# Dense layer pair with Silu: x transposes alone on SyncE's queue, w1 loads on ScalarE's

## The chip, the cores and the metric

The kernel runs on one core of a Trainium2 chip. The metric is the device time of one execution in microseconds. The median of three runs before the change is 126.39 us (125.19 to 127.03).

The engines: TensorE multiplies (in the profile PE, its weight loads PEld), ScalarE (ACT) does Silu and half of the copies out of PSUM, VectorE (DVE) the other copies, SyncE (SP) issues DMAs. ScalarE can issue DMAs too. SP's DMAs and ScalarE's go through two queues to the same 16 DMA engines. GpSimd (POOL) only sets four constants.

## The reference

```python
B, S, D, F = 1, 2048, 640, 1728     # bf16
h = einsum("bsd,df->bsf", x, w1)
h = silu(h)
out = einsum("bsf,fd->bsd", h, w2)
```

## The kernel before

x has 2048 rows of 640 values. The kernel cuts the rows into four chunks of 512, the 640 contraction columns into five tiles of 128 (index k), and the 1728 features into 13 tiles of 128 (index ft) and a rest of 64. The first product needs x with its contraction on the partitions, so x is loaded from memory by DMA transposes (`turn_x`, L107) into `xT`. w1 is loaded into `w1s` by plain copies (`load_w1`, L104), w2 into `w2s` and `w2t`.

The first stage has this order on TensorE:

- 13 dummy matmuls on a zeroed tile `z` (L134 to L137), 256 columns each, with no data from memory.
- The opening, chunk 0 with feature tiles 0 to 7 (L182 to L189): for each k, eight matmuls of 512 columns, one into each of the eight PSUM banks. So each k needs one tile of x (`ld_x[k]`, L184) and 1024 columns of w1 (`ld_w[k, 0]` and `ld_w[k, 1]`, L186). After the last k each bank goes through Silu on ScalarE (L169).
- The rest of chunk 0, feature tiles 8 to 12, with the five k of one bank in a row (L190 to L196). It waits for `ld_wr` (L146), the load of the w1 columns from 1024 on, 880 KB: the w1 remainder.
- Chunks 1 to 3, 13 feature tiles each, each behind its transpose `ld_xc[c]` (L147, L191), then the feature rest (L198 to L204).

All matmuls of both products are recorded on line L165. The second product follows from 64 us on, with transposes and stores issued by SP (L249 to L317); the change doesn't touch it.

What orders the start is a start barrier: each engine reports to it with a Drain and waits for its release at an EventSemaphore. `early` (L89) moves instructions ahead of one of the two: with `arrived` False ahead of the engine's Drain, so that they delay its report, with True between Drain and EventSemaphore, where they go on while others have not reported. Before the change these are moved so:

- SP: `x0(0, 2)`, the transpose of x tiles 0 and 1 of chunk 0, ahead of the Drain (L118); behind the Drain `sp_front` (L122 to L129), in this order: w1 tile k=0 second half, w1 k=1, x tiles 2 and 3, w1 k=2, w1 k=3, x tile 4, w1 k=4. After the barrier follow the w1 remainder, the transposes of chunks 1 to 3 and four w2 loads (L146 to L153).
- ScalarE: the first half of w1 tile k=0 (L132), behind its Drain; after the barrier a small Silu on a zeroed tile (L143, L144), which brings the load of the activation table with it.
- VectorE: the two memsets (L119, L120), ahead of its Drain.
- TensorE: the dummies, behind its Drain (L141). The opening comes after the barrier.

Each DMA has a semaphore of its own (`dma_sem`), and all matmuls that report share `s_pe`.

Of the kernel before, what the change touches and what calls it, by code (L numbers as in the profile page):

```python
# [5 lines left out]
ACT = mybir.ActivationFunctionType  # L6
ET = mybir.EngineType


def bass_standalone__dense_activation_silu__prompt_kernel(  # L10
# [12 lines left out]
    F = w1.shape[1]  # L23
    P = 128
    NB = 8
    BANK = 512
    DT = D // P
# [7 lines left out]
    FO = 8  # L35
    assert (S, D, F) == (2048, 640, 1728) and FL == 64

    pe, act, dve, sp = nc.tensor, nc.scalar, nc.vector, nc.sync

    with ExitStack() as es:  # L40
        def sb(name, shape, dtype):
            return es.enter_context(nc.sbuf_tensor(name, shape, dtype))

        xT = sb("xT", [P, DT, S], bf16)
        w1s = sb("w1s", [P, DT, F], bf16)
# [6 lines left out]
        z = sb("z", [P, 256], bf16)  # L52
        zw = sb("zw", [P, 8], fp32)
        ps = es.enter_context(nc.psum_tensor("ps", [P, NB, BANK], fp32))
# [3 lines left out]
        def sem(name):  # L58
            return [es.enter_context(nc.semaphore(name)), 0]

        def tick(ins, s, n=1):
            ins.then_inc(s[0], n)
            s[1] += n
            return (s, s[1])

        def wait(eng, *points):
            for pt in points:
                if pt is None:
                    continue
                s, v = pt  # L70
                key = (id(eng), id(s))
                if seen.get(key, 0) < v:
                    eng.wait_ge(s[0], v)
                    seen[key] = v

        s_pe, s_act, s_dve = sem("s_pe"), sem("s_act"), sem("s_dve")
        n_dma = [0]

        def dma_sem():
            n_dma[0] += 1  # L80
            return sem(f"s_dma{n_dma[0]}")

        def load(eng, out_ap, in_ap):
            return tick(eng.dma_start(out=out_ap, in_=in_ap), dma_sem(), 16)
# [4 lines left out]
        def early(emit, engine, arrived):  # L89
            lst = nc.main_func.blocks[0].instructions  # L90
            n = len(lst)
            r = emit()
            lst = nc.main_func.blocks[0].instructions
            new = lst[n:]
            del lst[n:]
            op = "EventSemaphore" if arrived else "Drain"
            at = next(i for i, ins in enumerate(lst) if ins.opcode == op and ins.engine == engine)
            lst[at:at] = new
            return r

        w1_v = w1.rearrange("(dt p) f -> p dt f", p=P)
        w2_v = w2[0:F0, :].rearrange("(ft p) d -> p ft d", p=P)

        def load_w1(eng, k, a, b):  # L104
            return load(eng, w1s[:, k, a * P:b * P], w1_v[:, k, a * P:b * P])

        def turn_x(c, k0, k1):  # L107
            return turn(sp, xT[:, k0:k1, c * SCH:(c + 1) * SCH],
                        xf[c * SCH:(c + 1) * SCH, k0 * P:k1 * P])

        ld_x, ld_w = {}, {}

        def x0(k0, k1):
            r = turn_x(0, k0, k1)
            for k in range(k0, k1):
                ld_x[k] = r

        early(lambda: x0(0, 2), ET.SP, False)  # L118
        p_z = early(lambda: tick(dve.memset(z[:, :], 0.0), s_dve), ET.DVE, False)  # L119
        p_zw = early(lambda: tick(dve.memset(zw[:, :], 0.0), s_dve), ET.DVE, False)  # L120

        def sp_front():  # L122
            ld_w[0, 1] = load_w1(sp, 0, 4, 8)
            ld_w[1, 0] = ld_w[1, 1] = load_w1(sp, 1, 0, 8)
            x0(2, 4)
            ld_w[2, 0] = ld_w[2, 1] = load_w1(sp, 2, 0, 8)
            ld_w[3, 0] = ld_w[3, 1] = load_w1(sp, 3, 0, 8)
            x0(4, 5)
            ld_w[4, 0] = ld_w[4, 1] = load_w1(sp, 4, 0, 8)  # L129

        def act_front():
            ld_w[0, 0] = load_w1(act, 0, 0, 4)  # L132

        def dummies(n):  # L134
            wait(pe, p_z)
            for _ in range(n):
                pe.matmul(ps[:, NB - 1, 0:256], lhsT=z[:, 0:P], rhs=z[:, :], start=True, stop=True)  # L137

        early(act_front, ET.Activation, True)
        early(sp_front, ET.SP, True)  # L140
        early(lambda: dummies(13), ET.PE, True)  # L141

        wait(act, p_zw)  # L143
        act.activation(out=zw[:, :], in_=zw[:, :], func=ACT.Silu)  # L144

        ld_wr = load(sp, w1s[:, :, FO * P:F], w1_v[:, :, FO * P:F])  # L146
        ld_xc = {c: turn_x(c, 0, DT) for c in range(1, NSC)}  # L147
        ld_w2 = [
            load(sp, w2s[:, 0:7, :], w2_v[:, 0:7, :]),
# [8 lines left out]
        def bank():  # L158
            b = nxt[0] % NB
            nxt[0] += 1  # L160
            wait(pe, bank_free[b])
            return b

        def mm(o, l, r, start, stop, shared=False):
            return pe.matmul(o, lhsT=l, rhs=r, start=start, stop=stop, skip_group_check=shared)  # L165

        def silu(out_ap, b, after):
            wait(act, after)
            r = tick(act.activation(out=out_ap, in_=ps[:, b, :], func=ACT.Silu), s_act)  # L169
            bank_free[b] = r  # L170
            return r

        def hcol(ft, c):
            return hT[:, ft, c * SCH:(c + 1) * SCH]

        def xcol(k, c):
            return xT[:, k, c * SCH:(c + 1) * SCH]

        def w1t(k, ft):
            return w1s[:, k, ft * P:(ft + 1) * P]  # L180

        obank = [bank() for _ in range(FO)]  # L182
        for k in range(DT):
            wait(pe, ld_x[k])  # L184
            for ft in range(FO):
                wait(pe, ld_w[k, ft // 4])  # L186
                ins = mm(ps[:, obank[ft], :], w1t(k, ft), xcol(k, 0), start=(k == 0), stop=(k == DT - 1))
                if k == DT - 1:
                    silu(hcol(ft, 0), obank[ft], tick(ins, s_pe))  # L189
        for c in range(NSC):  # L190
            wait(pe, ld_wr if c == 0 else ld_xc[c])  # L191
            for ft in range(FO if c == 0 else 0, FT):
                b = bank()
                for k in range(DT):
                    ins = mm(ps[:, b, :], w1t(k, ft), xcol(k, c), start=(k == 0), stop=(k == DT - 1))
                h_last = silu(hcol(ft, c), b, tick(ins, s_pe))  # L196
        h_tail = []
        for q in range(NSC // 2):  # L198
            b = bank()
            for k in range(DT):  # L200
                for hh in range(2):
                    ins = mm(ps[hh * FL:(hh + 1) * FL, b, :], w1s[:, k, F0:F], xcol(k, 2 * q + hh),
                             start=(k == 0), stop=(k == DT - 1), shared=True)
# [142 lines left out]
```

## Time and profile before

| what | us |
|---|---|
| median of three runs (lowest, highest) | 126.39 (125.19, 127.03) |
| profiled execution, its own time | 126.76 |
| its span, first to last instruction | 125.3 |
| TensorE matmuls busy | 121.6 (97%) |
| weight loads busy | 55.1 |
| ScalarE busy | 38.3 |
| VectorE busy | 7.6 |
| opening's first matmul starts | 3.70 |
| rest of chunk 0 starts | 14.47 |
| first product's last chunk ends, second product starts | about 64.3 |
| last matmul ends | 123.4 |

The issues on SP's queue in the first microseconds, from its timeline, and the landings from the DMA issues of narrow windows:

| issued at | what | KB | issue took | lands after |
|---|---|---|---|---|
| 0.00 | transpose x tiles 0, 1 | 256 | 1.34 | 3.7 |
| 1.83 | w1 k=0 second half, w1 k=1 | 128, 256 | 0.84 both | 2.9, 3.2 |
| 2.72 | transpose x tiles 2, 3 | 256 | 1.23 | 3.7 |
| 3.99 | w1 k=2, k=3 | 256 each | 1.05 both | 4.3, 4.4 |
| 5.09 | transpose x tile 4 | 128 | 1.15 | 4.5 |
| 6.29 | w1 k=4, w1 remainder | 256, 880 | 1.10 both | 3.9, 7.4 |
| 7.43 | transposes of chunks 1, 2, 3 | 640 each | 14.00 all | 9.9 the first, 5.8 the last |

ScalarE's one load was issued at 0.20 and landed 2.4 us later. Its table load starts at 1.98 and takes 1.28, the small Silu 0.21.

A matmul's busy time contains its drain, which the next one overlaps: the distance from start to start is less than the mean duration. An idle time in brackets behind a group names what ended it. A profile's group can merge instructions of several shapes ("+1 forms").

### The profile page before, as it was taken

The numbers are of one execution on the slowest core, as the hardware profiler recorded it, in microseconds if no ns is written. First come the engines' busy times: TensorE is split into PE (matmuls) and PEld (weight loads), VectorE is DVE, ScalarE is ACT, GpSimd is POOL, SyncE is SP. The second block draws the span as 40 slices with busy tenths as digits, with TensorE's granted clock in tenths as the row PEclk, the third lists the DMA queues.
The fourth block names the chain that finished last, engine by engine and source line by source line (L and its number), as shares of the span: only waits on it lengthen the run. The fifth ranks groups of instructions, "written<-read, shape, count | busy, mean of one in ns | idle before, by whom it ended". The sixth has DMA issues, their size and how long they took to land.

```text
span 125.3 us, 1333 instructions
## 1 busy us (share of the span) xinstructions
PE 121.6 (97%) x587; PEld 55.1 (44%) x587; DVE 7.6 (6%) x13; ACT 38.3 (31%) x66; POOL 0.2 (0%) x4
## 2 busy tenths in 40 slices
PE   8899799999999999999999999999999999999993
PEld 5334344444444444444434444444444444444452
DVE  0000000000000000000002020200004210012021
ACT  3100975555555555555540101010003011010100
POOL 0000000000000000000000000000000000000000
DMA  6999699995000000000000000000001468111113
GB/s 130 230 236 344 146 213 154 274 373 182 0 0 0 0 5 0 3 0 0 0 0 0 5 0 0 0 0 0 0 0 42 89 218 295 52 52 52 52 55 102
DMA packets 18437, 10.35 MB, mean 83 GB/s; under 512 B 13056, under 2 KB 17920, under 8 KB 18432
## 3 DMA queue, kind: packets, MB, share of 16 engines
q1 hardware_dynamic: 18144, 10.08, 31.5%
q10 hardware_dynamic: 288, 0.20, 0.7%
q8 instruction: 4, 0.07, 0.2%
q14 instruction: 1, 0.01, 0.0%
HBM read 4.51 MB, written 2.62 MB: 57 GB/s over the span
## 4 chain that ended last, share of the span: by engine, by line
PE 87%; DMA 6%; ACT 0%; issue 0%
PE ps L165 87%; DMA w1s<-in_w_dram 6%; ACT o_sb L215 0%
## 5 line engine op out<-in xcount | busy, mean ns | idle before, releaser
L165 PE MATMUL ps<-xT,w1s 128*128 128x512 bf16 (+1 forms) x280 | 59.7, 383 | 1.3 <-DMA w1s<-in_w_dram 1.0
L165 PE MATMUL ps<-w2s,hT 128*128 128x512 bf16 (+2 forms) x221 | 45.4, 367 | 0.0
L165 PEld LDWEIGHTS ps<-xT,w1s 128*128 128x128 bf16 (+1 forms) x280 | 26.5, 99 | 34.6 <-issue 1.5
L169 ACT ACTIVATE hT<-ps 128x512 bf16<-128x512 f32 x52 | 30.2, 603 | 29.1 <-PE ps L165 29.0
L165 PEld LDWEIGHTS ps<-w2s,hT 128*128 128x128 bf16 x221 | 20.9, 98 | 24.4 <-issue 1.1
L215 ACT CAST o_sb<-ps 128x512 bf16<-128x512 f32 (+1 forms) x8 | 4.4, 545 | 41.8 <-PE ps L165 41.8
L213 DVE CAST o_sb<-ps 128x512 bf16<-128x512 f32 (+1 forms) x9 | 6.1, 677 | 101.4 <-PE ps L165 101.4
L165 PE MATMUL ps<-hT,w2s 128*128 128x512 bf16 x52 | 11.4, 379 | 0.0
L165 PEld LDWEIGHTS ps<-hT,w2s 128*128 128x128 bf16 x52 | 5.1, 98 | 6.1
L215 ACT CAST oT<-ps 128x512 bf16<-128x512 f32 x2 | 1.1, 589 | 11.4 <-PE ps L165 11.4
L137 PE MATMUL ps<-z 128*128 128x256 bf16 x13 | 3.0, 416 | 0.4 <-DVE zw L120 0.4
L165 PE MATMUL ps<-w2t,hTt 64*128 64x512 bf16 (+2 forms) x17 | 2.3, 367 | 0.0
L137 PEld LDWEIGHTS ps<-z 128*128 128x128 bf16 x13 | 1.8, 142 | 1.1 <-DVE zw L120 0.4
L213 DVE CAST oT<-ps 128x512 bf16<-128x512 f32 x2 | 1.3, 686 | 14.1 <-PE ps L165 14.1
L144 ACT ACT_TABLE_LOAD x1 | 1.3, 1283 | 2.0 <-PEq L331 2.0
L169 ACT ACTIVATE hTt<-ps 128x512 bf16<-128x512 f32 x2 | 1.2, 597 | 1.1 <-PE ps L165 1.1
L165 PEld LDWEIGHTS ps<-w2t,hTt 64*128 64x128 bf16 x17 | 0.6, 94 | 1.6 <-issue 1.3
L165 PE MATMUL ps<-hTt,w2t 64*128 64x512 bf16 x4 | 0.6, 376 | 0.0
L165 PEld LDWEIGHTS ps<-hTt,w2t 64*128 64x128 bf16 x4 | 0.2, 94 | 0.2
L144 ACT ACTIVATE zw<-zw 128x8 f32<-128x8 f32 x1 | 0.2, 208 | 0.0
L119 DVE MEMSET z<- 128x128 uint32 x1 | 0.2, 165 | 0.2 <-issue 0.2
L331 POOL MEMSET const-bfloat16-1.0<- 128x1 bf16 x1 | 0.1, 101 | 0.0
(4 smaller groups left out, 0.4 us busy)
## 6 DMA issues: line engine op xcount, KB each, us to landing
out_dram<-o_sb SPq DMA_DIRECT2D x15, 160.0 KB, 1.9
w2s<-in_w_dram SPq DMA_DIRECT2D x1, 1120.0 KB, 6.7
w1s<-in_w_dram SPq DMA_DIRECT2D x4, 256.0 KB, 4.1
w2s<-in_w_dram SPq DMA_DIRECT2D x1, 960.0 KB, 8.8
w1s<-in_w_dram SPq DMA_DIRECT2D x1, 880.0 KB, 7.4
w2t<-in_w_dram SPq DMA_DIRECT2D x2, 80.0 KB, 8.1
w1s<-in_w_dram ACTq DMA_DIRECT2D x1, 128.0 KB, 2.4
w1s<-in_w_dram SPq DMA_DIRECT2D x1, 128.0 KB, 2.9
```

What stands on the lines that cost most here:

```text
L119: p_z = early(lambda: tick(dve.memset(z[:, :], 0.0), s_dve), ET.DVE, False)
L137: pe.matmul(ps[:, NB - 1, 0:256], lhsT=z[:, 0:P], rhs=z[:, :], start=True, stop=True)
L144: act.activation(out=zw[:, :], in_=zw[:, :], func=ACT.Silu)
L165: return pe.matmul(o, lhsT=l, rhs=r, start=start, stop=stop, skip_group_check=shared)
L169: r = tick(act.activation(out=out_ap, in_=ps[:, b, :], func=ACT.Silu), s_act)
L213: r = tick(dve.tensor_copy(out=out_ap, in_=in_ap), s_dve)
L215: r = tick(act.copy(out=out_ap, in_=in_ap), s_act)
L331: nc = _bacc.Bacc("TRN2", target_bir_lowering=False, num_devices=1)
```

## The change

- SP issues `x0(0, 1)`, `x0(1, 3)` and `x0(3, 5)` one after another, all ahead of its Drain, and no w1 load. After the barrier it waits for the w1 remainder before it issues the transposes of chunks 1 to 3 and the w2 loads.
- ScalarE issues all w1 loads behind its Drain. The first half of k=0 goes at once, all others behind `s_pe` 1, which the fourth dummy now raises. Then, still ahead of the barrier's EventSemaphore, the small Silu with its table load. After the barrier it issues the w1 remainder.
- TensorE runs 12 dummies in place of 13, and the opening's first four k stand ahead of the barrier's EventSemaphore too; the last k comes after it.

```diff
-        early(lambda: x0(0, 2), ET.SP, False)
+        def sp_front():
+            x0(0, 1)
+            x0(1, 3)
+            x0(3, 5)
+
+        def act_front():
+            ld_w[0, 0] = load_w1(act, 0, 0, 4)
+            wait(act, (s_pe, 1))
+            ld_w[0, 1] = load_w1(act, 0, 4, 8)
+            for k in range(1, DT):
+                ld_w[k, 0] = ld_w[k, 1] = load_w1(act, k, 0, 8)
+            act_table()
+
+        def act_table():
+            wait(act, p_zw)
+            act.activation(out=zw[:, :], in_=zw[:, :], func=ACT.Silu)
+
+        def dummies(n):
+            wait(pe, p_z)
+            for i in range(n):
+                ins = pe.matmul(ps[:, NB - 1, 0:256], lhsT=z[:, 0:P], rhs=z[:, :], start=True, stop=True)
+                if i == 3:
+                    tick(ins, s_pe)
+
+        early(sp_front, ET.SP, False)
         p_z = early(lambda: tick(dve.memset(z[:, :], 0.0), s_dve), ET.DVE, False)
         p_zw = early(lambda: tick(dve.memset(zw[:, :], 0.0), s_dve), ET.DVE, False)
-
-        def sp_front():
-            ld_w[0, 1] = load_w1(sp, 0, 4, 8)
-            ld_w[1, 0] = ld_w[1, 1] = load_w1(sp, 1, 0, 8)
-            x0(2, 4)
-            ld_w[2, 0] = ld_w[2, 1] = load_w1(sp, 2, 0, 8)
-            ld_w[3, 0] = ld_w[3, 1] = load_w1(sp, 3, 0, 8)
-            x0(4, 5)
-            ld_w[4, 0] = ld_w[4, 1] = load_w1(sp, 4, 0, 8)
...
         early(act_front, ET.Activation, True)
-        early(sp_front, ET.SP, True)
-        early(lambda: dummies(13), ET.PE, True)
-
-        wait(act, p_zw)
-        act.activation(out=zw[:, :], in_=zw[:, :], func=ACT.Silu)
-
-        ld_wr = load(sp, w1s[:, :, FO * P:F], w1_v[:, :, FO * P:F])
+
+        ld_wr = load(act, w1s[:, :, FO * P:F], w1_v[:, :, FO * P:F])
+        wait(sp, ld_wr)
         ld_xc = {c: turn_x(c, 0, DT) for c in range(1, NSC)}
...
+        def opening(k0, k1):
+            for k in range(k0, k1):
+                wait(pe, ld_x[k])
+                for ft in range(FO):
+                    wait(pe, ld_w[k, ft // 4])
+                    ins = mm(ps[:, obank[ft], :], w1t(k, ft), xcol(k, 0), start=(k == 0), stop=(k == DT - 1))
+                    if k == DT - 1:
+                        silu(hcol(ft, 0), obank[ft], tick(ins, s_pe))
+
+        def pe_front():
+            dummies(12)
+            opening(0, DT - 1)
+
+        early(pe_front, ET.PE, True)
+        opening(DT - 1, DT)
```

More of the change, by code (lines that the diff above doesn't have):

```diff
@@ L116, in x0 @@
                 ld_x[k] = r
-        early(lambda: x0(0, 2), ET.SP, False)
+        def sp_front():
[19 more added lines that the diff above has]
+        early(sp_front, ET.SP, False)
         p_z = early(lambda: tick(dve.memset(z[:, :], 0.0), s_dve), ET.DVE, False)
         p_zw = early(lambda: tick(dve.memset(zw[:, :], 0.0), s_dve), ET.DVE, False)
-        def sp_front():
-            ld_w[0, 1] = load_w1(sp, 0, 4, 8)
-            ld_w[1, 0] = ld_w[1, 1] = load_w1(sp, 1, 0, 8)
-            x0(2, 4)
-            ld_w[2, 0] = ld_w[2, 1] = load_w1(sp, 2, 0, 8)
-            ld_w[3, 0] = ld_w[3, 1] = load_w1(sp, 3, 0, 8)
-            x0(4, 5)
-            ld_w[4, 0] = ld_w[4, 1] = load_w1(sp, 4, 0, 8)
[L131 to L137, printed above, removed]
-        early(act_front, ET.Activation, True)
-        early(sp_front, ET.SP, True)
-        early(lambda: dummies(13), ET.PE, True)
-        wait(act, p_zw)
-        act.activation(out=zw[:, :], in_=zw[:, :], func=ACT.Silu)
-        ld_wr = load(sp, w1s[:, :, FO * P:F], w1_v[:, :, FO * P:F])
+        early(act_front, ET.Activation, True)
+        ld_wr = load(act, w1s[:, :, FO * P:F], w1_v[:, :, FO * P:F])
+        wait(sp, ld_wr)
         ld_xc = {c: turn_x(c, 0, DT) for c in range(1, NSC)}
@@ L182, in bass_standalone__dense_activation_silu__prompt_kernel @@
         obank = [bank() for _ in range(FO)]
[L183 to L189, printed above, removed]
+        def opening(k0, k1):
[11 more added lines that the diff above has]
+        opening(DT - 1, DT)
         for c in range(NSC):
```

## The prediction

> **What bounds the kernel now.** I read the chain of work that ended last first, then the groups of instructions, then TensorE's timeline, then the table of stages, then the DMA issues. The chain is short:
>
> ```profile
> by line: PE ps L165 86.9%; DMA w1s<-in_w_dram 5.9%; ACT o_sb L215 0.2%; issue 0.1%
> 6.94 0.06 issue
> 7.00 7.43 DMA w1s<-in_w_dram
> 14.43 0.05 issue
> 14.47 108.90 PE ps L165 x533
> 123.37 0.02 issue
> 123.40 0.27 ACT o_sb L215
> ```
>
> Columns: start, length, what. From 14.47 us to 123.37 us TensorE works without a break. What comes before 14.47 is the only part in which time can be won: the end moves by as much as that instant moves. It is the landing of one load, the w1 remainder (feature tiles 8 to 13), issued at 7.00.
>
> ```profile
> L165 PE MATMUL ps<-xT,w1s 128*128 128x512 bf16 (+1 forms) x280 | 59.7, 383 | 1.3 <-DMA w1s<-in_w_dram 1.0
> L144 ACT ACT_TABLE_LOAD x1 | 1.3, 1283 | 2.0 <-PEq L331 2.0
> ```
>
> Of all idle time ahead of first-stage matmuls, 1.3 us in total, most ends with a w1 load. TensorE's timeline (start, length, what, idle time before) shows where:
>
> ```profile
> 0.39 2.95 PE L137 MATMUL ps<-z 128*128 128x256 bf16 x13 [0.39 <-DVE zw L120]
> 3.70 4.46 PE L165 MATMUL ps<-xT,w1s 128*128 128x512 bf16 x16 [0.35 <-DMA xT<-in_x_dram]
> 8.39 5.34 PE L165 MATMUL ps<-xT,w1s 128*128 128x512 bf16 x24 [0.23 <-DMA w1s<-in_w_dram]
> 14.47 11.83 PE L165 MATMUL ps<-xT,w1s 128*128 128x512 bf16 x54 [0.74 <-DMA w1s<-in_w_dram]
> ```
>
> 24 matmuls take 5.34 us with a drain of about 0.16 after the last, so one goes every 0.2155 us. The 16 before take 4.46. The weight loads say why: they start at 4.10, 4.53, 4.95 and 5.38, 0.425 apart, and the next 11 take 2.28 us. So the array is slow until about 5.4 us, although the granted clock is recorded as 1.00 throughout: four matmuls at 0.425, twelve at 0.2155. The opening of 40 matmuls at full pace is 8.6 us; it starts at 3.70 and the next stage starts at 14.47, so 2.1 us of that stretch go to the slow start (4 x 0.21 = 0.84), 0.23 and 0.74 of waits, and drains.
>
> The table of stages (columns: window, its length, busy us of PE, PEld, DVE, ACT and POOL, clock, DMA share, GB/s) gives transfer rates:
>
> ```profile
> 9.00:10.00 1.00, 1.00 (x6) 0.49 (x5) 0.00 (x0) 0.00 (x0) 0.00 (x0) 1.00 1.01 306
> 10.00:11.00 1.00, 1.00 (x7) 0.41 (x5) 0.00 (x0) 0.00 (x0) 0.00 (x0) 1.00 1.04 366
> 12.00:13.00 1.00, 1.00 (x7) 0.47 (x5) 0.00 (x0) 0.74 (x2) 0.00 (x0) 1.00 2.77 155
> 13.00:14.00 1.00, 0.73 (x4) 0.12 (x2) 0.00 (x0) 1.00 (x3) 0.00 (x0) 1.00 0.15 31
> 15.00:16.00 1.00, 1.00 (x7) 0.41 (x6) 0.00 (x0) 1.00 (x3) 0.00 (x0) 1.00 1.28 290
> ```
>
> Copies alone (the w1 remainder, 10 to 11) run at 366 GB/s, transposes alone (15 to 16) at 290. Between 13 and 14 only 31 GB/s move: the last packets of the w1 remainder trickle, and the chunk-1 transposes queued behind it hardly advance. That is how a transpose can stand still beside an unfinished copy.
>
> **The change, part by part.** The sum is against the profiled execution: span 125.3, time 126.76, 0.37 above the median of the runs, 126.39. I subtract gains from the median too.
>
> *First transpose of one tile instead of two.* Issues on SP cost 1.34 and 1.23 for two tiles and 1.15 for one (timeline of SP). The two-tile transpose landed 3.7 after its issue at 0. One tile saves about 0.2 of issue and 128 KB, 0.45 us at 290 GB/s: it lands at about 3.0. The floor is TensorE itself: one dummy fewer (2.95 becomes about 2.74 busy, the next instruction can start at 2.95). I take 3.0 instead of 3.70; bounds 2.95 and 3.7. If the clock still steps up at 5.4, contraction tile 0 has 5.6 slow matmuls and 2.4 fast ones: it ends at 5.9 (before: 8 matmuls from 3.70 end at 6.3). Most of the 0.7 us is spent on slow matmuls.
>
> *w1 loads on ScalarE's queue behind dummy 4.* That dummy ends near 0.39 + 4 x 0.213 + drain = 1.4 to 1.5. Then five issues at the 0.42 of the L84 row: 1.5 to 3.6. The first ACT load was issued at 0.20 and landed 2.4 later. So tile 0's second half, issued at 1.5, lands about 3.9, wanted at 3.0 + 4 x 0.425 = 4.7: hidden, and if it took the 4.4 of the slowest small w1 load, 5.9, it would cost 1.2. Tile 1, issued at 1.9, lands between 4.3 and 6.3 (2.4 to 4.4); wanted at 5.9. Tiles 2 to 4 are issued 0.42 apart and wanted 1.72 apart, so they are hidden behind matmuls. All five cost nothing under that cover.
>
> *Transposes alone on SP's queue.* x tiles 1 and 2 are issued at 1.15, tiles 3 and 4 at about 2.4. This is the disputed price, since before has no stretch where long copies and transposes run from two queues. Lower bound: 3.7 from issue as for tiles 0 and 1, so 4.85, hidden behind tile 0. The nearest row is the second transpose of before, landing 3.7 after issue with 384 KB of copies ahead of it in its own queue; beside this one run 640 KB (half of tile 0, tiles 1 and 2), 256 KB or 0.7 us more: 5.6. Upper bound, if the engines give each queue one packet in turn: copies of 1152 KB from 2.5 on are 640 packets and take 3.2 us, 640 of the transpose's 1024 packets go between them (0.57 us), the other 384 after (0.34), plus 0.45 from the last packet to the landing (as for the first transpose: 3.2 and 3.65): 7.1; 8.6 if the w1 remainder already fills the gaps. I take the midpoint of 5.6 and 7.1, because the remainder can't be in flight that early (next part): 6.4, and TensorE resumes at 6.5, a wait of 0.6. Tiles 3 and 4 then have until 6.5 + 16 x 0.2155 = 9.95, 7.5 us after their issue: hidden. The opening ends at 6.5 + 32 x 0.2155 = 13.4.
>
> *The w1 remainder on ScalarE.* It is behind the start barrier. ScalarE's idle time before its table load ended at 1.98, 0.64 after SP's transpose issue ended at 1.34: SP's Drain comes last. With three transposes ahead, that is 1.15 + 1.23 + 1.23 + 0.64 = 4.25. The table load and the small Silu (1.28 + 0.21) now stand before the barrier, from 3.6 on; they hold the load until 5.1 if the queue waits for them, not at all if it doesn't. Issue at 4.25 to 5.1, against 7.00. With the 7.4 of its own row it lands at 11.7 to 12.5; at 366 GB/s alone it would be near 9. Either is before 13.4, so the 0.74 wait at the end of the opening goes; cover left, about 1 us. The table load itself is wanted for the first Silu, at 12.26 before and near 11.7 after: hidden.
>
> *SP waits for the remainder before chunk 1.* Queued behind are the transposes of chunks 1 to 3, four w2 loads and, much later, stores. Chunk 1 is wanted 25 matmuls (5.4 us) after the opening, at 18.8. Issue at 12.5 at the latest, first packets 1.6 later (as for the transpose issued at 0), 640 KB at 290 GB/s 2.3 us (before it took nearer 3), landing near 17.5; cover 1.3. Chunks 2 and 3 are wanted 14 us later each, w2 at 64: hidden. What is lost if the cover goes: the delay one for one.
>
> *Clock start.* Twelve dummies not thirteen, and 0.35 of idle time less: nothing, bounds -0.8 and +0.8 (four slow matmuls fewer or more). The Trainium skill, TensorE: Matmul & The Clock Gate (Part 1: The HAM clock gate), says that full clock comes after one busy window of some 3.4 us and that the window runs freely. By that an estimate could place the step as early as 3.8 here, and the sum would be 0.8 less wherever tile 0 sets the pace; the trace's step at 5.4 fits a free window, not a fixed count.
>
> **Sum.** Start of the second stage 14.47 to 13.4: -1.1 us. The rest, 108.9 us of matmuls and the last store, is unchanged. 126.76 - 1.1 = 125.7 for a run like the profiled one, 126.39 - 1.1 = 125.3 for the median.
>
> **Rivals.**
>
> *No mutual delay.* Transposes land by 5.9 and nothing waits: 5.9 + 32 x 0.2155 = 12.8, -1.65, 124.7. For it: between 1.8 and 2.2 us the DMA view shows 62 packets of ScalarE's queue beside 202 of SP's, and the transpose went on. Against: that copy was 128 KB only.
>
> *Strict turns.* One packet each, with the w1 remainder filling in: x tiles 1 and 2 land at 8.6, wait 2.8, opening ends 8.7 + 6.9 = 15.6: +1.1, 127.5. For it: the packets here are 256 bytes against 2 KB, so equal turns starve the transpose. The Trainium skill, DMA: Bandwidth & Descriptors (Queues, rings and completion order), says that each DMA engine takes the queues in turn, packet by packet; no stretch of this trace is long enough to show it for large copies.
>
> *Slower: transposes stand still until the copies are through,* as they nearly did from 12.4 to 14.3. w1 drains by 8.2 (1152 KB and 880 KB at 366 from 2.5, no gap) or, with a trickle of 1.9 as in that stretch, 10.1; then 0.9 for x tiles 1 and 2 (256 KB at 290) and 0.45 to land: 9.5 to 11.5. TensorE resumes at 10.6 in the middle, the opening ends at 17.5: +3.0, 129.4. It is slower than before as soon as x tiles 1 and 2 land after 7.6, and by over 2% after 10.1. Against it: before's trickle was within one queue, which two queues may mend.
>
> *Faster by more:* the clock is up when tile 0 starts and nothing waits, 3.0 + 8.6 = 11.6: -2.85, 123.5.
>
> **How the numbers follow.** Forecast 0.40, no mutual delay 0.24, strict turns 0.19, standstill 0.13, early clock 0.04. About 2% (2.5 us) is what a measurement of this kernel can tell from no change; the three runs before already lie 1.8 us apart. Forecast, no delay and strict turns lie within it: 0.83; standstill is slower, 0.13; early clock faster, 0.04. The range reaches from no delay (124.7) to strict turns (127.5), 0.83 of the chance, widened by 0.4 each side for the scatter of medians: 124.3 to 127.9. The forecast's own range is 124.7 to 126.0 (x tiles at 5.6 to 7.1).
>
> **What would show it.** Right: tile 0's first matmul at 3.0; a pause of about half a microsecond before matmul 9, ended by a transpose of x; no pause before the second stage, which starts near 13.4; w1 remainder issued at 4.3 to 5.1; chunk 1 landing before 18.8. Wrong: a pause of over 2 us before matmul 9 or 25 (turns or standstill), a pause before the second stage or before chunk 1 (remainder late), or slow weight-load spacing after 5.4.

## The result and the profile after

The change makes the kernel slower: 130.6 us median of four runs (130.53 to 131.53) against 126.51 for the kernel before (four runs, 125.19 to 127.03). The ratio is 1.036, 95% interval 1.032 to 1.041. The profiled execution after took 130.53, its span is 129.1: 3.8 more than before.

Line 167 is now the matmul helper, as line 165 was. TensorE's timeline after (start, length, what, idle time before it and what ended it):

```profile
0.39 2.74 PE L138 MATMUL ps<-z 128*128 128x256 bf16 x12 [0.39 <-DVE zw L144]
5.52 1.90 PE L167 MATMUL ps<-xT,w1s 128*128 128x512 bf16 x8 [2.38 <-DMA xT<-in_x_dram]
9.64 22.58 PE L167 MATMUL ps<-xT,w1s 128*128 128x512 bf16 x94 [2.22 <-DMA xT<-in_x_dram]
```

Two waits of over 2 us, both ended by a transpose of x, stand where before had 0.35 and 0.23. The wait for w1 at the second stage is gone, as is any later one. The second stage has its first weight load at 18.03; weight loads run one matmul ahead here, so its first matmul comes near 18.25 instead of 14.47. That is 3.8 later, the whole loss of the span, and from there all is as before. The chain that ended last names the transfer:

```profile
1.28 8.31 DMA xT<-in_x_dram
9.60 0.05 issue
9.64 8.12 PE ps L167 x29
```

The transpose of x tiles 1 and 2, issued at 1.28, lands 8.31 us later. The copies beside it are late too. In the DMA issues (queue, count, KB of one, median us to landing):

```profile
w1s<-in_w_dram ACTq DMA_DIRECT2D x4, 256.0 KB, 9.2
w1s<-in_w_dram ACTq DMA_DIRECT2D x1, 880.0 KB, 10.1
w1s<-in_w_dram ACTq DMA_DIRECT2D x2, 128.0 KB, 4.0
```

Before, a 256 KB load took 4.1 us and the 880 KB remainder 7.4. So nobody gained what the transposes lost. The table of stages says how much moved (window, length, busy us of PE, PEld, DVE, ACT and POOL, clock, DMA share, GB/s):

```profile
3.00:4.00 1.00, 0.13 (x1) 0.00 (x0) 0.00 (x0) 0.01 (x1) 0.00 (x0) 1.00 0.77 82
4.00:5.00 1.00, 0.00 (x0) 0.00 (x0) 0.00 (x0) 1.00 (x1) 0.00 (x0) 1.00 1.26 165
5.00:6.00 1.00, 0.48 (x3) 0.25 (x4) 0.00 (x0) 0.48 (x2) 0.00 (x0) 1.00 0.96 146
6.00:7.00 1.00, 1.00 (x6) 0.43 (x5) 0.00 (x0) 0.00 (x0) 0.00 (x0) 1.00 1.20 149
7.00:8.00 1.00, 0.42 (x2) 0.00 (x0) 0.00 (x0) 0.00 (x0) 0.00 (x0) 1.00 1.39 152
8.00:9.00 1.00, 0.00 (x0) 0.00 (x0) 0.00 (x0) 0.00 (x0) 0.00 (x0) 1.00 0.81 151
...
11.00:12.00 1.00, 1.00 (x4) 0.40 (x3) 0.00 (x0) 0.00 (x0) 0.00 (x0) 0.50 1.22 281
12.00:13.00 1.00, 1.00 (x4) 0.30 (x2) 0.00 (x0) 0.00 (x0) 0.00 (x0) 0.50 0.93 123
```

From 3 to 9 us, with both kinds in flight, 82 to 165 GB/s go through, where in single microseconds of the kernel before copies alone ran at 366 and transposes alone at 290. The DMA share is 0.77 to 1.39: packets are outstanding on the engines, but few bytes move. The last two lines show a second effect: the clock column falls to 0.50 at 11 to 13 us, with four matmuls a microsecond instead of six. By the clock records that stretch is 10.5 to 13.9 us and holds eight matmuls at 0.427.

### The profile page after: what moved, and what is told of

It reads as the page before. It is cut to its first block, busy times and chain, and to the rows that moved or that the text cites. A ratio compares the mean times of both kernels' runs of the same rounds, so it can differ in the third digit from the quotient of the medians.

```text
span 129.1 us, 1320 instructions
## 1 busy us (share of the span) xinstructions
PE 121.5 (94%) x575; PEld 55.2 (43%) x586; DVE 7.6 (6%) x13; ACT 38.1 (30%) x66; POOL 0.2 (0%) x4
## 4 chain that ended last, share of the span: by engine, by line
PE 91%; DMA 6%; SPq 1%; issue 1%; ACT 0%
PE ps L167 91%; DMA xT<-in_x_dram 6%; SPq L87 1%; ACT o_sb L226 0%
## 6 DMA issues: line engine op xcount, KB each, us to landing
w1s<-in_w_dram ACTq DMA_DIRECT2D x1, 880.0 KB, 10.1
```

## The experiments

Theory A: a DMA transpose and plain copies that run side by side from two queues hold each other up. Theory B: it is the grouping 1, 2, 2 and the amount put in flight, whichever queue it is in. Landings below without a fence are the last of a DMA's 16 semaphore reports in the trace, from the one profiled execution of each kernel. "Second stage" is the first weight load of the rest of chunk 0.

### One queue

The w1 loads go back to SP, between the transposes; SP's first transpose stays ahead of the Drain, the rest is behind it.

```diff
         def sp_front():
             x0(0, 1)
+
+        def sp_next():
+            ld_w[0, 1] = load_w1(sp, 0, 4, 8)
+            ld_w[1, 0] = ld_w[1, 1] = load_w1(sp, 1, 0, 8)
             x0(1, 3)
+            ld_w[2, 0] = ld_w[2, 1] = load_w1(sp, 2, 0, 8)
+            ld_w[3, 0] = ld_w[3, 1] = load_w1(sp, 3, 0, 8)
             x0(3, 5)
+            ld_w[4, 0] = ld_w[4, 1] = load_w1(sp, 4, 0, 8)
...
-            wait(act, (s_pe, 1))
-            ld_w[0, 1] = load_w1(act, 0, 4, 8)
-            for k in range(1, DT):
-                ld_w[k, 0] = ld_w[k, 1] = load_w1(act, k, 0, 8)
...
-        ld_wr = load(act, w1s[:, :, FO * P:F], w1_v[:, :, FO * P:F])
+        early(sp_next, ET.SP, True)
+
+        ld_wr = load(sp, w1s[:, :, FO * P:F], w1_v[:, :, FO * P:F])
```

> All loads of the start but the first w1 half tile go through SP's queue, in the order x tile 0, w1 k=0 second half, w1 k=1, x tiles 1 and 2, w1 k=2 and k=3, x tiles 3 and 4, w1 k=4, w1 remainder. Theory A (transposes and copies from two queues hold each other up on the DMA engines): the same bytes in one queue land as before the change, x tiles 1 and 2 within 4 us of their issue and w1 loads within 4.5 us, no slow clock, 126 to 127 us. Theory B (it is the grouping 1, 2, 2 and the amount of bytes in flight, whichever the queue): x tiles 1 and 2 land after 8 us again and the time stays at 129 to 131 us.

Measured: 125.87 us, just under the 126 to 127 of theory A, ratio to before 1.000 (0.997 to 1.003). TensorE's timeline in this kernel:

```profile
3.36 2.39 PE L171 MATMUL ps<-xT,w1s 128*128 128x512 bf16 x8 [0.23 <-DMA xT<-in_x_dram]
6.19 12.53 PE L171 MATMUL ps<-xT,w1s 128*128 128x512 bf16 x57 [0.44 <-DMA xT<-in_x_dram]
18.98 13.34 PE L171 MATMUL ps<-xT,w1s 128*128 128x512 bf16 x61 [0.26 <-DMA xT<-in_x_dram]
```

The waits are 0.23 and 0.44 us where the changed kernel has 2.38 and 2.22, and 0.26 for chunk 1. Grouping, dummies, moved opening and SP's wait for the remainder are those of the change. What differs is the queue of the copies and, with it, their order and moment: they stand between the transposes and no longer wait for dummy 4, and the second and third transposes come behind SP's Drain. Its 256 KB loads took 3.7 us (9.2 in the changed kernel):

```profile
w1s<-in_w_dram SPq DMA_DIRECT2D x4, 256.0 KB, 3.7
```

From 3 to 9 us it moves 178 to 311 GB/s, three of the stages being these:

```profile
4.00:5.00 1.00, 1.00 (x5) 0.41 (x4) 0.00 (x0) 0.00 (x0) 0.00 (x0) 1.00 1.08 311
5.00:6.00 1.00, 0.75 (x4) 0.14 (x2) 0.00 (x0) 0.00 (x0) 0.00 (x0) 1.00 1.28 207
6.00:7.00 1.00, 0.81 (x4) 0.41 (x5) 0.00 (x0) 0.00 (x0) 0.00 (x0) 1.00 0.81 268
```

Theory B falls as the whole explanation, since the same grouping costs nothing here. This run changes queue, order and moment of the copies together; the next ones hold them apart.

### Plain copies in place of the transposes

```diff
-            r = turn_x(0, k0, k1)
             for k in range(k0, k1):
-                ld_x[k] = r
+                ld_x[k] = load(sp, xT[:, k, 0:SCH].rearrange("p (a c) -> p a c", c=P),
+                               xf[0:SCH, k * P:(k + 1) * P].rearrange("(a p) c -> p a c", p=P))
```

> The changed kernel with chunk 0 of x brought by plain copies of 256-byte rows, one per contraction tile, in place of the DMA transposes: x is not transposed there, so chunk 0's product is another one; bytes, packet size and queues are as they were. Theory A1 (it is the transpose that clashes with copies): all x tiles and w1 loads land within 3 to 5 us of their issue, TensorE waits under 1 us, 124 to 126 us. Theory A2 (any two queues with small and large packets clash): x tiles 1 and 2 land after 7 us, 129 us or more.

Each x tile has a load of its own here, five in place of three transposes. Measured: 125.52 us, ratio to before 0.997 (0.994 to 1.000). Stages of this kernel:

```profile
3.00:4.00 1.00, 0.76 (x4) 0.32 (x4) 0.00 (x0) 0.19 (x1) 0.00 (x0) 1.00 0.74 186
4.00:5.00 1.00, 0.40 (x2) 0.00 (x0) 0.00 (x0) 1.00 (x1) 0.00 (x0) 1.00 1.09 330
5.00:6.00 1.00, 0.59 (x3) 0.31 (x4) 0.00 (x0) 0.30 (x2) 0.00 (x0) 1.00 1.18 312
6.00:7.00 1.00, 1.00 (x7) 0.34 (x5) 0.00 (x0) 0.00 (x0) 0.00 (x0) 1.00 1.07 378
```

Two queues, 256-byte packets in one and rows of 1 and 2 KB in the other, and 186 to 378 GB/s go through, in each stage at least twice what the changed kernel moved. Many loads took longer than the expected 3 to 5 us (x tile 2 landed at 6.44, 5.4 after its issue; w1 k=4 at 9.29, 6.0 after), and TensorE waited 1.01 us for w1 where I had expected less than 1, but the second stage starts at 13.0. It is the transpose that clashes, neither the packet size nor the second queue.

The DMA view shows where the rate goes. By queue (q10 is ScalarE's, q1 SP's), its columns are packets, MB and the time that the packets took, as a share of 16 engines. The changed kernel from 5 to 9 us:

```profile
q10 hardware_dynamic: 218, 0.41, 64.7%
q1 hardware_dynamic: 770, 0.19, 44.3%
```

This kernel, with plain copies only, from 4 to 7 us:

```profile
q10 hardware_dynamic: 421, 0.74, 70.0%
q1 hardware_dynamic: 1128, 0.28, 41.6%
```

Worked out from these rows, a copy packet took 0.19 us beside the transposes (0.647 x 16 x 4 us / 218) and 0.08 us beside plain copies, both at about 1.8 KB a packet; a packet of x took 0.037 and 0.018 us. So the packets of both queues take more than twice as long.

### All transposes first, in one queue, and the same in two queues

The first kernel issues x tiles 0, 1 and 2, 3 and 4 and then, behind the Drain, all w1 loads but the first on SP, the remainder too; the second keeps ScalarE's queue and changes the gate:

```diff
-            wait(act, (s_pe, 1))
-            ld_w[0, 1] = load_w1(act, 0, 4, 8)
+            act_table()
+
+        def sp_next():
+            ld_w[0, 1] = load_w1(sp, 0, 4, 8)
             for k in range(1, DT):
-                ld_w[k, 0] = ld_w[k, 1] = load_w1(act, k, 0, 8)
-            act_table()
+                ld_w[k, 0] = ld_w[k, 1] = load_w1(sp, k, 0, 8)
...
-        ld_wr = load(act, w1s[:, :, FO * P:F], w1_v[:, :, FO * P:F])
+        early(sp_next, ET.SP, True)
+
+        ld_wr = load(sp, w1s[:, :, FO * P:F], w1_v[:, :, FO * P:F])
```

```diff
-            wait(act, (s_pe, 1))
+            wait(act, ld_x[DT - 1])
```

> All three transposes first and then all w1 loads but the first half tile, on SP's one queue, so that no copy runs beside a transpose. Theory A (two queues hold each other up): x tiles land near 3.0, 4.6 and 6.0 us, w1 k=1 lands at 8 to 9 us and TensorE waits for w1 only; 127 to 129 us. Theory B (amount in flight): x tiles 1 and 2 late as in the changed kernel, over 8 us, and 130 us or more.

> The changed kernel, two queues, but all w1 loads except the first half tile wait for the landing of x tiles 3 and 4 instead of for dummy 4, so that no copy runs beside a transpose. Theory A (it is the running side by side that costs): x tiles land by 3.5, 5.2 and 6.5 us, each w1 load within 4.5 us of its issue, the last of them (k=4) by 12 us instead of 14.2. TensorE still loses, now to w1 (k=0 second half lands near 8.5): 128 to 131 us. Rival A3 (two queues are slow by themselves, in whatever order): w1 loads land 7 us or more after issue and the last after 14 us.

Measured: 129.82 us, ratio 1.031 (1.024 to 1.037), and 131.05, ratio 1.042 (1.035 to 1.050). The transfers came near to what theory A said: x tiles at 4.2, 5.0 and 6.2 in the first, 4.1, 5.3 and 6.4 in the second, and w1 k=4 at 11.2 and 13.1 instead of 14.2; the first tile of each and w1 k=4 of the second are 0.6 to 1.2 later than I had expected. In the second kernel the w1 loads behind the gate landed 2.1 to 4.9 us after issue, so two queues are not slow by themselves. Its stages from 3 to 6 us hold the transposes and, until 3.8, the end of the first half tile:

```profile
3.00:4.00 1.00, 0.13 (x1) 0.00 (x0) 0.00 (x0) 0.00 (x0) 0.00 (x0) 1.00 1.05 176
4.00:5.00 1.00, 0.83 (x3) 0.28 (x4) 0.00 (x0) 0.00 (x0) 0.00 (x0) 1.00 1.03 166
5.00:6.00 1.00, 1.00 (x3) 0.15 (x1) 0.00 (x0) 0.00 (x0) 0.00 (x0) 1.00 0.71 146
```

So the transposes of chunk 0, issued back to back, move 146 to 176 GB/s by themselves, not the 290 of chunk 1's stretch before the change. The copies beside them in the changed kernel added nothing to that: 82 to 165 GB/s for both. One kind after the other, w1 k=4 is through at 13.1 although the gate opens only at 6.4; side by side it took until 14.2.

The time missed my expectation for the first, 127 to 129, and lies at the upper end of it for the second, 128 to 131. Both lose to w1, whose second half of k=0 landed at 7.5 and 8.5, and to the clock: 13 and 17 distances between matmuls, start to start, are 0.40 to 0.43 us. The clock column stays at 1.00 in both, so here only the distances show it.

### The clock

Two runs fill TensorE's idle stretches with matmuls of zeros, one in the changed kernel, one in the kernel that has all transposes first.

```diff
-            dummies(12)
-            opening(0, DT - 1)
+            dummies(28)
+            opening(0, 1)
+            zeros(20)
+            opening(1, DT - 1)
...
```

```diff
...
+                    if k == 0 and ft == 4:
+                        zeros(12)
                     wait(pe, ld_w[k, ft // 4])
...
-            dummies(12)
+            dummies(18)
...
```

> The changed kernel with 28 dummies instead of 12 and 20 matmuls of zeros, added to one bank, between contraction tiles 0 and 1, so that TensorE has no idle window; the transfers are as they were. Theory: of the 3.8 us lost, 1.7 are eight matmuls at half clock after the wait that ends at 9.6 us; with the array kept busy the slow stretch at 10.5 to 13.9 us is gone and the time is near 128.9 us. Rival (the slow stretch comes whatever TensorE does, or the wait hides it): 130.6 us again.

> The one-queue kernel with all transposes first, plus work of zeros that keeps TensorE busy: 18 dummies instead of 12, and 12 matmuls of zeros added to one bank while it waits for the second half of w1 k=0. That kernel landed everything by 11.2 us and still took 129.8. Theory: 2.4 us of it are slow clock after idle stretches; with them filled it is 127 to 128 us, what is left being the wait for w1. Rival (the slow stretch has no part in it): 129.5 us or more.

Measured: 130.86 us for the first, ratio 1.038 (1.032 to 1.044): no gain, my expectation fell. The slow stretch is gone, but a wait stands in its place:

```profile
6.89 2.35 PE L167 MATMUL ps<-z 128*128 128x256 bf16 x20
10.14 3.63 PE L167 MATMUL ps<-xT,w1s 128*128 128x512 bf16 x16 [0.90 <-DMA xT<-in_x_dram]
15.45 16.79 PE L167 MATMUL ps<-xT,w1s 128*128 128x512 bf16 x77 [1.69 <-DMA xT<-in_x_dram]
```

x tiles 3 and 4 landed at 15.4 here and at 14.2 in the changed kernel. There, as an estimate, tile 2 would have ended at 9.64 + 16 x 0.2155 = 13.1 at full clock and TensorE would have waited until 14.25; slowed, it went on at 14.58. So of the 1.7 us of slow matmuls about 0.3 count. Where nothing is late next, the clock does count: the second kernel took 128.34 (ratio 1.017, 1.012 to 1.022), 1.5 less than unfilled, with no slow matmul left, although its second half of k=0 landed 0.7 later. I had expected 127 to 128.

### How much beside it

Three kernels hold w1 loads until x tiles 1 and 2 have landed: all of k=2 to 4, the same with w1 cut into 1 KB rows, and all of k=1 to 4.

```diff
             for k in range(1, DT):
+                if k == 2:
+                    wait(act, ld_x[1])
                 ld_w[k, 0] = ld_w[k, 1] = load_w1(act, k, 0, 8)
```

> The changed kernel, two queues, with the w1 loads k=2, 3 and 4 held until x tiles 1 and 2 have landed; beside those tiles run 384 KB of copies instead of up to 1152 KB. Theory A, the price grows with what runs beside: x tiles 1 and 2 land at 5.5 to 7.5 us instead of 9.6, second stage at 15 to 16.5, 127 to 129 us. Rival A4 (any overlap costs the same stall): they land at 9 us or later and the time is 130 us or more.

Against that kernel, the one with the short rows:

```diff
-                ld_w[k, 0] = ld_w[k, 1] = load_w1(act, k, 0, 8)
+                ld_w[k, 0] = load_w1(act, k, 0, 4)
+                ld_w[k, 1] = load_w1(act, k, 4, 8)
```

> As the run that holds k=2 to 4 until x tiles 1 and 2 have landed (384 KB of copies beside them, landing at 9.2 us), but each w1 load of k=1 to 4 is cut into two of 1 KB rows, as the k=0 halves are. Theory P (the long 2 KB packets beside 256-byte transpose packets make the stall): x tiles 1 and 2 land by 7 us. Rival Q (it is the amount and the time side by side, whatever the row length): 8.5 us or later again.

Against the changed kernel again:

```diff
+            wait(act, ld_x[1])
             for k in range(1, DT):
                 ld_w[k, 0] = ld_w[k, 1] = load_w1(act, k, 0, 8)
```

> The changed kernel with the w1 loads k=1 to 4 held until x tiles 1 and 2 have landed, so that only 128 KB of copies (second half of k=0) run beside them. Theory A with a price by amount: x tiles 1 and 2 land at 6 to 7 us (5.3 with no copy beside, 9.2 with 384 KB). Rival A4 (any overlap costs the whole stall): 8.5 us or later.

Measured: 129.87 us (ratio 1.032, 1.027 to 1.037), 129.82 (1.027, 1.024 to 1.030) and 128.11 (1.015, 1.010 to 1.020). The chain of each shows the transpose of x tiles 1 and 2, in this order:

```profile
1.29 7.91 DMA xT<-in_x_dram
```

```profile
1.29 6.99 DMA xT<-in_x_dram
```

```profile
1.28 4.43 DMA xT<-in_x_dram
```

| copies that may run beside x tiles 1 and 2, beyond the first half of w1 k=0, which every kernel loads from 0.2 us on | they land at |
|---|---|
| none (all transposes first, two queues) | 5.3 |
| 128 KB | 5.7 |
| 384 KB, k=1 in 1 KB rows | 8.3 |
| 384 KB, k=1 in 2 KB rows | 9.2 |
| 1152 KB (as changed) | 9.6 |

I had expected the price to grow with the amount and 5.5 to 7.5 for 384 KB; the rival said that any overlap costs the whole. Neither fits: 128 KB cost 0.4 us, 256 KB more cost 3.5, all the rest 0.4. Only the step of 3.5 is clear of scatter: x tiles 1 and 2 landed at 5.0 and 5.5 in the two kernels with all transposes first in one queue, whose transfers are the same, and at 9.5 and 10.1 in two others whose transfers at that point are as changed (the fill above, and the one without SP's wait below). In every row from 384 KB on, w1 k=1 lands within 0.3 us of the transpose (9.0, 8.5 and 9.4): both crawl and end together. The stages of the 384 KB kernel with 2 KB rows:

```profile
3.00:4.00 1.00, 0.14 (x1) 0.00 (x0) 0.00 (x0) 0.00 (x0) 0.00 (x0) 1.00 1.02 110
4.00:5.00 1.00, 0.00 (x0) 0.00 (x0) 0.00 (x0) 0.00 (x0) 0.00 (x0) 1.00 1.03 168
5.00:6.00 1.00, 0.96 (x3) 0.42 (x4) 0.00 (x0) 0.00 (x0) 0.00 (x0) 1.00 1.26 126
6.00:7.00 1.00, 1.00 (x4) 0.32 (x3) 0.00 (x0) 0.00 (x0) 0.00 (x0) 1.00 1.11 106
7.00:8.00 1.00, 1.00 (x4) 0.30 (x2) 0.00 (x0) 0.00 (x0) 0.00 (x0) 1.00 1.19 137
```

106 to 168 GB/s, with nothing in flight but the transposes (the first until 5.0) and, after the first half tile's landing at 3.2, at most 384 KB of copies. With the short rows the landing came 0.9 us earlier, one execution against one; 8.3 is under the 8.5 that the rival set and over the 7 of the theory, so that run decides for neither.

### The grouping and SP's wait

```diff
-            x0(0, 1)
-            x0(1, 3)
-            x0(3, 5)
+            x0(0, 2)
+            x0(2, 4)
+            x0(4, 5)
```

> The changed kernel with x of chunk 0 in transposes of 2, 2 and 1 tiles as before the change; queues, gates and order otherwise as changed. Theory A: the grouping is not the cause, the transposes still run beside the w1 loads, 129.5 to 132 us. Theory B (grouping 1, 2, 2 puts more behind the second transpose and makes the loss): 126 to 128 us.

```diff
-        wait(sp, ld_wr)
```

> The changed kernel without SP's wait for the w1 remainder, so that chunk 1's transposes queue right behind x tiles 3 and 4 and run beside the remainder. Theory A: the wait costs nothing (chunk 1 landed 1.8 us before it was wanted), and without it the remainder lands later, at 17 us or more instead of 16.4; 130 to 132 us. Rival (the wait is a part of the loss): 128 us or less.

Measured: 127.98 us for the grouping 2, 2, 1, with runs from 127.03 to 129.94, ratio 1.016 (1.009 to 1.022): below what theory A expected, inside what B did. In two queues the grouping is worth some 2.6 us, more than half of the loss; in one queue the grouping 1, 2, 2 cost nothing (first experiment). So theory A alone does not give the size. The one execution that was profiled is the slowest of the four, 129.94 us (the others took 127.03 to 128.24). In it x tiles 0 and 1 landed at 3.9, x tiles 2 and 3 at 10.6 and w1 k=1 at 9.2, so the stall is there with this grouping too, behind two tiles of x that are in hand. What the faster runs gain, no trace shows; I leave it open. Without SP's wait: 131.1, ratio 1.042 (1.037 to 1.048), no better than changed. Its remainder landed at 18.1 instead of 16.4 and chunk 1 at 20.0 instead of 21.8. Neither is late: the second stage starts at 18.2, and chunk 1 is wanted 5.4 after that.

### A version to beat both

The one-queue kernel without SP's wait, which the order of one queue makes needless.

```diff
-        wait(sp, ld_wr)
```

> The one-queue kernel with 1, 2, 2 contraction tiles, without SP's wait for the w1 remainder, which the queue's order makes needless. There chunk 1 landed at 18.93 us and TensorE waited 0.26 us for it, while the second stage began about 13.1 instead of 14.47. Theory: the transposes of chunk 1 follow the remainder at once, land by 18 us, nothing waits after the opening, and the time is 0.3 to 1.5 us under the kernel before, 124.5 to 125.7. Rival: chunk 1's descriptors beside the last packets of the remainder hold it up as before the change (landing at 14.4), and the time equals before.

Measured: 126.03 us, above the 124.5 to 125.7 that I had expected, ratio to the kernel before 0.997 (0.995 to 1.000). TensorE's timeline:

```profile
3.56 28.76 PE L170 MATMUL ps<-xT,w1s 128*128 128x512 bf16 x127 [0.42 <-DMA xT<-in_x_dram]
```

From 3.56 on there is no wait left, and chunk 1 lands at 16.1. Its transposes stand right behind the remainder in the queue, as before the change, and from 12 to 14 us 230 and 290 GB/s move where before had 155 and 31: the trickle of before does not come with that order alone. Still the gain can't be told from none: beside it the kernel before took 126.38 (125.28 to 126.87). The profiled execution of before, 126.76, lay near the upper end of its own scatter, so part of the waits seen there may not be in every run; no other execution of it was profiled.

## Why the prediction was wrong

It said 125.3, with a range of 124.3 to 127.9; 130.6 was measured.

- *What bounds the kernel.* Right: the second stage's first matmul comes 3.8 us later, the span is 3.8 longer, and the rest is unchanged.
- *The step that failed: "Transposes alone on SP's queue".* I put x tiles 1 and 2 at 6.4, between 5.6 (one queue, with the extra copies at their own rate) and 7.1 (packets in turn). They landed at 9.6, past the 8.6 that I gave for turns with the remainder filling in. Both ends took for granted that the engines' time is shared and none is lost. The runs show loss: 82 to 165 GB/s while both run from 3 to 9 us, 178 to 311 there with the same transfers in one queue, and 186 to 378 from 3 to 7 us with the same bytes as plain copies. The 290 GB/s by which I priced a transpose was not reached either where three were issued back to back: they moved 146 to 176 with no copies beside them. x tiles 3 and 4, which I called hidden and wanted at 9.95, landed at 14.2, 1.1 after tile 2 would have ended at full clock.
- *The rule of turns.* The Trainium skill, DMA: Bandwidth & Descriptors (Queues, rings and completion order), says that each engine takes the queues in turn, packet by packet. The Trainium skill counts a packet there as some 9 to 17 descriptors. My estimate took one packet of the profile, 256 bytes or 2 KB, for it, and no run here shows how the two relate. The estimate, 7.1 to 8.6, does not agree with 9.6, nor with 9.2 when only 384 KB could run beside. Turns, as I priced them, share the engines' time and lose none of it, so turns alone don't make the loss.
- *First transpose.* Wrong, and past the bound of 3.7: it landed at 5.47, and tile 0 started at 5.52 instead of 3.0. It landed at 3.3 and 3.5 in the two one-queue kernels with copies between the transposes, at 4.1 to 4.2 with only transposes behind it, and at 4.6 to 5.5 in the six kernels that kept the change's first transpose and had copies in ScalarE's queue from dummy 4 on.
- *w1 loads hidden.* Wrong for the same reason: 9.2 us each instead of 2.4 to 4.4; w1 k=4 landed at 14.2 like x tiles 3 and 4.
- *w1 remainder.* Issued at 6.32, not 4.25 to 5.1, since the third transpose's issue took 3.05 us instead of 1.23 and SP's Drain stands behind it (2.61 + 3.05 + 0.64 = 6.30). It landed at 16.4, later than I said, and is hidden before 18.0; the 0.74 wait is gone.
- *SP's wait.* Right: chunk 1 landed at 21.8, wanted at 23.4, cover 1.6 (I said 1.3); taking the wait away gained nothing.
- *Clock start.* I allowed 0.8 either way at the beginning. Tile 0 ran at full pace, but a slow stretch came later, after the waits, 10.5 to 13.9. The Trainium skill, TensorE: Matmul & The Clock Gate (Part 1: The HAM clock gate), gives windows of some 3.4 us; this stretch, 3.41 us in the clock records, agrees. In this kernel it cost little, since x tiles 3 and 4 landed later than tile 2 would have ended without it.
- *Rivals.* The standstill, 129.4 with a chance of 0.13, came nearest in time, and its 9.5 to 11.5 for x tiles 1 and 2 holds the 9.6 measured. Its mechanism is half right: the transposes do crawl, but the copies crawl with them.

Open: by what the engines lose the time when a transpose and copies run side by side from two queues. The runs show that it needs a transpose, that it needs side by side, that it sets in between 128 and 384 KB of copies and that the single packets take longer; not what they wait for. Open too is why the grouping 2, 2, 1 loses so much less.

## What to carry to other kernels

Keep sizeable plain copies in a second queue away from DMA transposes; a second queue beside a transpose is no free issue slot. What cost nothing here was to put the copies into the transposes' own queue, between them, in the order in which TensorE wants them (125.87 and 126.03 us). Holding them until a transpose has landed speeds the transfers up, but TensorE then waits for the copies: 131.05 us with all held, 128.11 with k=1 to 4 held. Price two kinds of transfer in flight together by a stretch that shows them together, and if there is none, allow for a combined rate below that of either. When a stall appears, ask what lands next before counting the clock's share: filling the idle time gained 1.5 us in one kernel and nothing in the other.

## What the runs showed of the hardware

Transposes and copies side by side from two queues moved 82 to 165 GB/s in the stages from 3 to 9 us. The same transfers in one queue, the copies between the transposes, moved 178 to 311 in these stages, and plain copies of the same packet sizes in two queues 186 to 378 from 3 to 7 us. Three transposes issued back to back, without those copies beside them, moved 146 to 176 from 3 to 6 us. The onset is steep: x tiles 1 and 2 landed at 5.7 us with 128 KB of copies beside the 256 KB transpose, which can't be told from 5.3 with none, and at 9.2 with 384 KB. The issue of the third transpose on SP, 256 KB, took 1.30 us in the three kernels with no copies beside it but the first half tile, 1.98 with 128 KB more, 2.32 to 2.75 with 384 KB and 2.74 to 3.05 with up to 1152 KB.
